# Two attention blocks, forward and backward: K and V loads from SyncE's queue to GpSimd's, dO*O from GpSimd to VectorE

## The chip, the core and the metric

The kernel runs on one core of a Trainium2 chip. The metric is device time in microseconds of one execution. The five engines that matter here are TensorE (PE in the profile; PEld are its weight loads), VectorE (DVE), ScalarE (ACT), GpSimd (POOL) and SyncE (SP, which computes nothing and issues DMAs). Each engine works through its own list of instructions in order. A DMA is issued by SP or by POOL and then carried by the core's DMA engines; a DMA that must wait, for a buffer or for data, holds up what stands behind it on the engine that issues it.

## The reference

Two independent attention blocks, A and B, each with its own x, K cache, V cache, wq and wo. The outputs are the two results side by side and the gradients of all ten inputs.

```python
def block(x, k_cache, v_cache, wq, wo):      # x 8x96x640, caches 8x32x512x128, all bf16
    q = (x @ wq).reshape(B, Sq, H, Dh).transpose(0, 2, 1, 3)
    scores = einsum("bhqd,bhkd->bhqk", q, k_cache) * Dh ** -0.5
    p = softmax(scores)
    o = einsum("bhqk,bhkd->bhqd", p, v_cache)
    return o.transpose(0, 2, 1, 3).reshape(B, Sq, H * Dh) @ wo
out, vjp = jax.vjp(lambda *inputs: concatenate([block(A...), block(B...)]), *inputs)
return out, *vjp(grad_out)
```

There are 8 batch rows (B), 96 queries (Sq), 32 heads (H), 512 keys (Sk) and 128 columns a head (Dh), so a block has 256 pairs of head and batch row, and the kernel 512. For each pair the forward pass needs S = QK^T, P = softmax(S), O = PV; the backward pass needs dV = P^T dO, dP = dO V^T, dS = P * (dP - rowsum(dO * O)), dQ = dS K and dK = dS^T Q. K and V are read once, 64 MB for each block, and dK and dV are written once.

## The kernel before

The kernel is a software pipeline written out by hand. Time is counted in ticks, and each tick starts one pair of head h and batch row b: pair b of head h has the base tick `ct = c0t + b`, with `c0t = tick0 + 8 h`. Block B follows block A without a break in the count. The function `build_block` puts every piece of work into a list with a tick and, inside the tick, a slot; the list is sorted by both and emitted in that order. The table `OFF` (L45) says how many ticks before or after `ct` a piece is due, and `SLOTS` (L51) its place inside the tick. A scheduler may then still move instructions of an engine, except those wrapped in `pinned(...)`, which keep the order of the program on their engine. The softmax pieces have a raised priority.

What one pair goes through:

- `c_ld` (L262) loads K and V. One load brings two batch rows (NB = 2), 256 KB, so K and V have one load each every two ticks. All are issued by SP. K's tile `K_sb` has 7 buffers and is due at tick -5 from its first row's `ct`; V's tile `V_sb` has 5 and is due at tick -3. Both stand in slot 0, the first of the tick. A buffer can be loaded again when its last reader is done: for K the dQ matmuls, 8 ticks after `ct`, for V the O matmuls, 5 ticks after it.
- `c_xt` (L272) transposes a tile on the way, by a DMA that SP issues. V always goes this way (`VT`, 4 buffers, tick 0). K goes this way (`KT`, 2 buffers, tick -3) for half of the pairs; for the others, and for the first heads, `k_on_pe` (L548) leaves it to TensorE: `c_s1` (L280) makes four transposes at tick +2, and VectorE copies the result (`KT_pe`).
- `c_s2a` and `c_s2b` (L291, L304), tick +3: S on TensorE, its row maximum `negm` on VectorE, the exponential `E_sb` on ScalarE.
- `c_s3a` and `c_s3b` (L315, L324), tick +3: `rinv` on VectorE, then `P_sb` on POOL, pinned.
- `c_s4` and the second half of `c_s45` (L382, L352), tick +4: dV, and the four transposes of P, which ScalarE copies to `PT_sb`.
- the first half of `c_s45`, tick +5: O, four matmuls with V; ScalarE copies it into `OD`, together with the dQ of another pair.
- `c_s5b` (L401), tick +5, slot 54: `prod`, the product of O and dO for this pair, 128 x 96, on POOL, pinned.
- `c_s6` (L411), tick +6: dP, with `VT`; `dl_ps`, the sum of `prod` over its 128 rows, by a matmul with ones; then `dS_sb` on VectorE from both and P.
- `c_s7`, tick +7: dK; `c_s8` (L333): four transposes of dS at tick +7 (`dst_ps`, copied to `dST_sb` by VectorE), dQ at tick +8.
- `c_st` (L395): the stores of dV and dK, two batch rows each, issued by POOL, pinned, slot 54.3. One of the two falls on each tick.

Around the pairs there is work per head, spread over the eight ticks of a head: wq and wo tiles loaded by POOL (`pA`, `pA2`, slot 54.6), their transposes, q and dO of the head, dwo and dwq with their stores from POOL, and for every six heads the output projections. At the start of block B, SP also loads x and grad_out once more in row blocks (`ld_tmp`, L118, pinned).

So POOL's list in a plain tick is: P_sb, prod, one store. SP's list is: the loads and the DMA transposes in one order, plus the row blocks.

Of the kernel before, what the change touches and what calls it, by code (L numbers as in the profile page):

```python
# [8 lines left out]
ALU = mybir.AluOpType  # L9
# [32 lines left out]
SL_GRP = 95  # L42
SL_SETUP = 96

OFF = dict(ldk=-5, ldv=-3, kt=-3, vt=0, s2=3, s3=3, s4=4, s5=5, s6=6, s7=7, s8=8)  # L45
HK = dict(pA=-10, pA2=-9, pB=-3, pC0=[-2, 0], pC1=[-1, 0], pD1=1, pD0=2, qA0=18, qA1=17, qB=[19, 20], qD=[(18, 0, 2), (19, 2, 4), (21, 4, 5)])
EV = dict(pB0="act", pB1="dve", pC00="act", pC01="act", pC10="act", pC11="dve", pD0="dve", pD1="dve", qA0="act", qA1="dve", qB0="act", qB1="dve", qD="dve", gU="act")
GSPREAD0 = 9
# [2 lines left out]
SLOTS = dict(LOAD=0, S2A=5, S2B=5.5, S1=6, S8=10, S7=20, S5=30, S4=40, S6=50, S3A=52, S3B=53, S5B=54, HEAD=SL_HEAD, GRP=SL_GRP)  # L51


def build_block(tc, em, tick0, blk, x, kc, vc, wq, wo, g_all, out_all, dx, dk, dv, dwq, dwo, ident, ones, pools, HG=6, first=True, groups=None):
    nc = tc.nc
# [7 lines left out]
    KC = Sk // 128  # L63
    NB = 2
# [46 lines left out]
    def pinned(ins):  # L111
        return tc.keep_in_program_order(ins)
# [149 lines left out]
    def c_ld(h, b, n, bufs):  # L262
        def f():
            src = kc if n == "K" else vc
            X = kvp.tile([128, NB, KC, 128], BF16, name=n + "_sb", bufs=bufs)
            nc.sync.dma_start(X[:], src[b:b + NB, h].rearrange("b (p c) d -> p b c d", c=KC))
            for i in range(NB):
                st = CS.setdefault((blk, h, b + i), {})
                st[n + "_sb"], st[n + "_all"] = X[:, i], X
        return f  # L270
# [130 lines left out]
    def c_s5b(h, b):  # L401
        def f():
            st = CS[(blk, h, b)]
            hs = HS[(blk, h)]
            tok = slice(b * Sq, (b + 1) * Sq)
            prod = wk.tile([128, Sq], BF16, name="prod", bufs=3)
            pinned(nc.gpsimd.tensor_tensor(prod[:], hs["OT_h"][:, tok], hs["dOT_h"][:, tok], op=ALU.mult))  # L407
            st["prod"] = prod
        return f

# [141 lines left out]
    for g in range(NG):  # L552
        h0 = GH0[g]
        for hh in range(groups[g]):
            h = h0 + hh
# [16 lines left out]
            for b in range(B):  # L572
                ct = c0t + b
                if b % NB == 0:
                    em.add(tick0 - 12 if first and h == 0 and b == 0 else ct + OFF["ldk"], SLOTS["LOAD"], c_ld(h, b, "K", 7))
                    em.add(ct + OFF["ldv"], SLOTS["LOAD"], c_ld(h, b, "V", 5))
                    if not k_on_pe(h, b):
                        em.add(ct + OFF["kt"], SLOTS["LOAD"] + 1, c_xt(h, b, "KT", 2))
                    em.add(ct + OFF["vt"], SLOTS["LOAD"] + 1, c_xt(h, b, "VT", 4))
                if k_on_pe(h, b):  # L580
                    em.add(ct + 2, SLOTS["S1"], c_s1(h, b))
                em.add(ct + OFF["s2"], SLOTS["S2A"], c_s2a(h, b))
                em.add(ct + OFF["s2"], SLOTS["S2B"], c_s2b(h, b))
                em.add(ct + OFF["s3"], SLOTS["S3A"], c_s3a(h, b))
                em.add(ct + OFF["s3"], SLOTS["S3B"], c_s3b(h, b))
                em.add(ct + OFF["s5"], SLOTS["S5B"], c_s5b(h, b))
                if b % 2 == 1:
                    em.add(ct + OFF["s4"] + 1, 54.3, c_st(h, b, "v"))
                    em.add(ct + OFF["s7"] + 1, 54.3, c_st(h, b, "k"))
                em.add(ct + OFF["s4"], SLOTS["S4"], c_s4(h, b))  # L590
                for i, o in enumerate(("s8", "s7", "s5", "s4")):
                    SX.setdefault(ct + OFF[o], [None] * 4)[i] = (blk, h, b)
                em.add(ct + OFF["s6"], SLOTS["S6"], c_s6(h, b))
                em.add(ct + OFF["s7"], SLOTS["S7"], c_s7(h, b))
# [147 lines left out]
```

## Time and profile before

| what | value |
|---|---|
| runs | 1696.48, 1707.16, 1713.74 us; median 1707.16 |
| profiled execution, first to last instruction | 1699.8 us |
| mean granted TensorE clock | 0.998 |
| bytes moved by DMA | 423.05 MB, 249 GB/s |
| K and V loads | 512 of 256 KB, median 4.9 to 5.3 us from issue to landing |
| DMA transposes | 256 of V (median 6.1 us to landing), 122 of K (5.2 us) |
| dK and dV stores | 512 of 256 KB |
| prod on POOL | 512 of 360 ns |
| P_sb on POOL | 512 of 689 ns |

The profile is of one execution. "Span" is the time from its first to its last instruction; the runs are whole executions without the profiler. A page gives busy time by engine, the chain of work that ended last, and groups of instructions by source line, with their count, total and mean time and the idle time in front of them. In "L329 POOL P_sb" the number is the line of the kernel. An arrow in "out<-in" names what an instruction writes and reads; an arrow after a waiting instruction names what ended its wait. A DMA issued by POOL is listed as an instruction of POOL, and its time there is the time that POOL needs to issue it, not the time of the transfer; "to landing" runs from the issue to the arrival of the last byte.

### The profile page before, as it was taken

The numbers are of one execution on the slowest core, as the hardware profiler recorded it, in microseconds if no ns is written. First come the engines' busy times: TensorE is split into PE (matmuls) and PEld (weight loads), VectorE is DVE, ScalarE is ACT, GpSimd is POOL, SyncE is SP. The second block draws the span as 40 slices with busy tenths as digits, with TensorE's granted clock in tenths as the row PEclk, the third lists the DMA queues.
The fourth block names the chain that finished last, engine by engine and source line by source line (L and its number), as shares of the span: only waits on it lengthen the run. The fifth ranks groups of instructions, "written<-read, shape, count | busy, mean of one in ns | idle before, by whom it ended". The sixth has DMA issues, their size and how long they took to land.

```text
span 1699.8 us, 56567 instructions
## 1 busy us (share of the span) xinstructions
PE 1675.7 (99%) x22024; PEld 1343.8 (79%) x22024; DVE 1329.8 (78%) x3052; ACT 1405.2 (83%) x3518; POOL 1040.3 (61%) x1747
## 2 busy tenths in 40 slices
PE   8999999999999999999999999999999999999999
PEld 7877778778778778777778877887788778778876
DVE  6887678878788878787778876787788778878877
ACT  6998889869869869878768998897799679878975
POOL 3676567646647647656566764675576557656754
PEclk9999999999999999999999999999999999999999
DMA  9999999999999999999999999999899989999994
GB/s 256 252 259 250 258 225 260 262 242 243 262 221 252 268 238 259 225 251 237 281 256 269 273 270 248 238 289 248 218 261 276 237 221 261 281 217 240 263 247 141
DMA packets 600429, 423.05 MB, mean 249 GB/s; under 512 B 419360, under 2 KB 557984, under 8 KB 600160
## 3 DMA queue, kind: packets, MB, share of 16 engines
q1 hardware_dynamic: 546576, 242.08, 72.2%
q0 software_dynamic: 53584, 177.35, 32.7%
q8 instruction: 173, 2.83, 0.7%
q14 instruction: 96, 0.79, 0.2%
HBM read 161.09 MB, written 159.12 MB: 188 GB/s over the span
## 4 chain that ended last, share of the span: by engine, by line
PE 89%; DMA 4%; ACT 3%; issue 1%; DVE 1%; POOL 0%; SPq 0%; DVEq 0%; ACTq 0%; POOLq 0%
PE q_ps L243 12%; PE o_ps L512 12%; PE dwo_ps L470 6%; PE dV_ps L389 6%; PE dK_ps L432 6%; PE S_ps L298 6%; PE dP_ps L417 6%; PE dwq_ps L490 6%; PE x_ps L340 5%; PE x_ps L365 5%; PE dst_ps L346 5%; PE x_ps L359 5%; PE kT_ps L285 3%; PE n_ps L258 3%; PE nat_ps L455 2%; DMA VT<-V_sb 1%
## 5 line engine op out<-in xcount | busy, mean ns | idle before, releaser
L329 POOL TENSOR_SCALAR P_sb<-E_sb,rinv 96x512 bf16<-96x512 bf16 x512 | 352.6, 689 | 567.8 <-DVE rinv L320 559.2
L310 ACT ACTIVATE E_sb<-S_ps,negm 96x512 bf16<-96x512 f32 x512 | 351.0, 686 | 187.6 <-DVE negm L300 181.9
L421 DVE SCALAR_TENSOR_TENSOR dS_sb<-dP_ps,dl_ps,P_sb 96x512 bf16<-96x512 f32 x512 | 382.1, 746 | 60.9 <-PE dl_ps L419 54.6
L300 DVE TENSOR_REDUCE negm<-S_ps 96x1 f32<-96x512 f32 x512 | 347.6, 679 | 50.9 <-PE S_ps L298 46.6
L435 ACT ACTIVATE dK_sb<-dK_ps 128x512 bf16<-128x512 f32 x512 | 302.1, 590 | 63.4 <-PE dK_ps L432 56.5
L392 ACT ACTIVATE dV_sb<-dV_ps 128x512 bf16<-128x512 f32 x512 | 311.6, 609 | 0.0
L378 ACT ACTIVATE PT_sb<-x_ps 128x384 bf16<-128x384 bf16 x512 | 253.1, 494 | 0.0
L512 PEld LDWEIGHTS <-OD 128*128 128x128 bf16 x1536 | 132.2, 98 | 100.4 <-issue 1.0
L398 POOL DMA_DIRECT2D out_dram<-dV_sb x256 | 194.9, 761 | 11.8 <-issue 8.6
L398 POOL DMA_DIRECT2D out_dram<-dK_sb x256 | 195.0, 762 | 9.1 <-issue 4.4
L389 PE MATMUL dV_ps<-dOnat_h,P_sb 96*128 96x128 bf16 x2048 | 198.2, 219 | 0.8 <-DVE dOnat_h L160 0.6
L417 PE MATMUL dP_ps<-VT,dOT_h 128*96 128x512 bf16 x512 | 195.4, 382 | 3.0 <-DMA VT<-V_sb 3.0
L432 PE MATMUL dK_ps<-Qnat_h,dS_sb 96*128 96x128 bf16 x2048 | 198.1, 219 | 0.1
L407 POOL TENSOR_TENSOR prod<-OD,dOT_h 128x96 bf16<-128x96 bf16 x512 | 184.2, 360 | 13.8 <-ACT OD L375 12.6
L348 DVE COPY dST_sb<-dst_ps 128x384 bf16<-128x384 bf16 x512 | 177.1, 346 | 10.5 <-PE dst_ps L346 10.3
L365 PE MATMUL x_ps<-ident,P_sb 96*128 96x96 bf16 x2048 | 172.0, 205 | 0.8 <-POOL P_sb L329 0.3
L359 PE MATMUL x_ps<-PT_sb,V_sb 128*128 128x96 bf16 x2048 | 172.3, 206 | 0.2 <-ACT PT_sb L378 0.2
L346 PE MATMUL dst_ps<-ident,dS_sb 96*128 96x96 bf16 x2048 | 172.3, 206 | 0.2 <-DVE dS_sb L421 0.2
L340 PE MATMUL x_ps<-dST_sb,K_sb 128*128 128x96 bf16 x2048 | 171.0, 206 | 1.3 <-ACT dK_sb L435 0.8
L375 ACT ACTIVATE OD<-x_ps 128x192 bf16<-128x192 f32 (+1 forms) x515 | 167.9, 326 | 3.9 <-PE x_ps L340 3.9
L320 DVE RECIPROCAL rinv<-rowsum 96x1 f32<-96x1 f32 x512 | 79.9, 156 | 106.0 <-ACT E_sb L310 100.4
L340 PEld LDWEIGHTS <-K_sb 128*128 128x128 bf16 x2048 | 131.1, 98 | 25.1 <-issue 1.6
(84 smaller groups left out, 3744.4 us busy)
## 6 DMA issues: line engine op xcount, KB each, us to landing
out_dram<-dV_sb POOLq DMA_DIRECT2D x256, 256.0 KB, 5.2
out_dram<-dK_sb POOLq DMA_DIRECT2D x256, 256.0 KB, 5.3
K_sb<-in_A_k_cache_dram SPq DMA_DIRECT2D x128, 256.0 KB, 5.3
V_sb<-in_A_v_cache_dram SPq DMA_DIRECT2D x128, 256.0 KB, 5.2
K_sb<-in_B_k_cache_dram SPq DMA_DIRECT2D x128, 256.0 KB, 5.0
V_sb<-in_B_v_cache_dram SPq DMA_DIRECT2D x128, 256.0 KB, 4.9
out_dram<-dwo_sb POOLq DMA_DIRECT2D x63, 160.0 KB, 4.8
out_dram<-dwq_sb POOLq DMA_DIRECT2D x31, 320.0 KB, 6.1
```

The costliest lines, as they stand in the source:

```text
L300: nc.vector.tensor_reduce(negm[:], S_ps[:], axis=AX.X, op=ALU.max, negate=True)
L310: nc.scalar.activation(E_sb[:], st["S_ps"][:], ACT.Exp, bias=st["negm"][:], scale=1.0, accum_out=rowsum[:])
L329: pinned(nc.gpsimd.tensor_scalar(P_sb[:], st["E_sb"][:], st["rinv"][:], 0.0, op0=ALU.mult, op1=ALU.add))
L340: nc.tensor.matmul(dQT_ps, st["K_sb"][:, c, :], st["dST_sb"][:, c * Sq:(c + 1) * Sq], start=(c == 0), stop=(c == KC - 1))
L389: nc.tensor.matmul(dV_ps[:, c * 128:(c + 1) * 128], P_sb[:, c * 128:(c + 1) * 128], hs["dOnat_h"][:, b * 128:(b + 1) * 128], start=True, s ...
L392: nc.scalar.activation(SB[(blk, h, b // 2, "v")][:, b % 2], dV_ps[:], ACT.Identity, scale=1.0)
L398: pinned(nc.gpsimd.dma_start(dst[b - 1:b + 1, h].rearrange("b (p c) d -> p b (c d)", c=KC), SB.pop((blk, h, b // 2, which))[:]))
L417: nc.tensor.matmul(dP_ps[:], hs["dOT_h"][:, tok], st["VT"], start=True, stop=True)
L421: nc.vector.scalar_tensor_tensor(dS_sb[:], dP_ps[:], dl_ps[:, 0:1], st["P_sb"][:], op0=ALU.subtract, op1=ALU.mult)
L432: nc.tensor.matmul(dK_ps[:, c * 128:(c + 1) * 128], dS_sb[:, c * 128:(c + 1) * 128], hs["Qnat_h"][:, b * 128:(b + 1) * 128], start=True, s ...
L435: nc.scalar.activation(SB[(blk, h, b // 2, "k")][:, b % 2], dK_ps[:], ACT.Identity, scale=1.0)
L512: nc.tensor.matmul(o_ps[:], src[:, t * 128:(t + 1) * 128], rhs, start=(hh == 0), stop=(hh == groups[g] - 1))
```

## The change

The K and V loads are issued by POOL, pinned, instead of SP; the loads of head 0 of block A alone stay on SP and in slot 0. The others go from slot 0 to slot 54.4, that is, behind P_sb and the store of their tick and ahead of the wq and wo loads. V's loads are due at tick -4 instead of -3, K's stay at -5. `prod` is computed by VectorE and is not pinned. Which K tiles TensorE transposes does not change, nor do the numbers of buffers.

```diff
-OFF = dict(ldk=-5, ldv=-3, kt=-3, vt=0, s2=3, s3=3, s4=4, s5=5, s6=6, s7=7, s8=8)
+OFF = dict(ldk=-5, ldv=-4, kt=-3, vt=0, s2=3, s3=3, s4=4, s5=5, s6=6, s7=7, s8=8)
...
             X = kvp.tile([128, NB, KC, 128], BF16, name=n + "_sb", bufs=bufs)
-            nc.sync.dma_start(X[:], src[b:b + NB, h].rearrange("b (p c) d -> p b c d", c=KC))
+            v = src[b:b + NB, h].rearrange("b (p c) d -> p b c d", c=KC)
+            if first and h == 0:
+                nc.sync.dma_start(X[:], v)
+            else:
+                pinned(nc.gpsimd.dma_start(X[:], v))
...
             prod = wk.tile([128, Sq], BF16, name="prod", bufs=3)
-            pinned(nc.gpsimd.tensor_tensor(prod[:], hs["OT_h"][:, tok], hs["dOT_h"][:, tok], op=ALU.mult))
+            (nc.vector.tensor_tensor(prod[:], hs["OT_h"][:, tok], hs["dOT_h"][:, tok], op=ALU.mult))
...
                 if b % NB == 0:
-                    em.add(tick0 - 12 if first and h == 0 and b == 0 else ct + OFF["ldk"], SLOTS["LOAD"], c_ld(h, b, "K", 7))
-                    em.add(ct + OFF["ldv"], SLOTS["LOAD"], c_ld(h, b, "V", 5))
+                    sl = SLOTS["LOAD"] if first and h == 0 else 54.4
+                    em.add(tick0 - 12 if first and h == 0 and b == 0 else ct + OFF["ldk"], sl, c_ld(h, b, "K", 7))
+                    em.add(ct + OFF["ldv"], sl, c_ld(h, b, "V", 5))
```

## The prediction

> **What bounds the kernel now.** I read the page first, then the chain of waits stretch by stretch, then the list of who waits for whom, then SyncE's own waits. The page:
>
> ```profile
> span 1699.8 us, 56567 instructions
> ...
> PE 1675.7 (99%) x22024; PEld 1343.8 (79%) x22024; DVE 1329.8 (78%) x3052; ACT 1405.2 (83%) x3518; POOL 1040.3 (61%) x1747
> ...
> DMA  9999999999999999999999999999899989999994
> ...
> PE 89%; DMA 4%; ACT 3%; issue 1%; DVE 1%; POOL 0%; SPq 0%; DVEq 0%; ACTq 0%; POOLq 0%
> ```
>
> TensorE carries 89% of the chain that ended last. Its 99% busy alone would prove little, because a lone matmul's row holds its latency too (219 ns for 128 columns). But in the chain four matmuls of 128 columns take 0.22 us, 0.055 us each, so they run back to back. At that rate (2.4 columns a ns) all 22024 matmuls, each with its columns from the table of groups, take 1574 us. From each matmul's start to the next one's I summed what exceeds this: 121 us in the whole span. Nearly every stretch of 50 us holds 2 to 3.5 us of it, which no queue can give back. Five stretches hold more: 0 to 50 us 12.7 (start), 100 to 150 6.9, 150 to 200 4.5, 750 to 800 6.2, 800 to 850 9.4. Over 2.6 us, the last four together hold 16.6 us, 1.0% of the span: what better transfers could bring at most in this execution. The waits in them:
>
> ```profile
> PE dP_ps L417 <- DMA VT<-V_sb: 3.0, 2, 2.4
> ...
> PE tp_ps L134 <- DMA ld_tmp<-in_grad_out_dram: 2.7, 1, 2.7
> ...
> PE S_ps L298 <- DMA KT<-K_sb: 2.1, 1, 2.1
> ```
>
> Each row: microseconds in total, times, longest. TensorE waited 3.0 us for V's transposes (VT) and 2.1 us for K's, of 378 such transfers, and 2.7 us for a row block of grad_out where block B begins. Two of these stalls have a tail. After the VT wait that ended at 125.3 us the clock falls (stage, then its time, the busy times of PE, PEld, DVE, ACT and POOL, the granted clock, DMA):
>
> ```profile
> 125.00:130.00 5.00, 4.67 (x39) 3.69 (x40) 2.64 (x4) 1.59 (x3) 0.00 (x0) 0.66 1.16 311
> ```
>
> 0.66 over 5 us is 1.7 us lost. The stage 829 to 834 us, after the wait for grad_out, shows 0.66 too: 1.7 us more.
>
> SyncE issues loads and transposes in one order, and stands in it:
>
> ```profile
> SPq L275 <- DMA K_sb<-in_A_k_cache_dram: 169.4, 57, 9.0
> ```
>
> A K transpose waits there for its K tile (152.0 us more for block B's), and the next loads and V transposes wait behind it. VT lands 0.04 to 24.9 us ahead of its matmul, 11.9 in the median: enough nearly always.
>
> **The change part by part.** *Loads leave SyncE.* 504 of 512 loads (all but head 0 of block A) go to POOL. SyncE then holds the transposes and a few row blocks only, with nothing ahead of them but their own tile. On POOL a K load now follows P_sb and the dK store of tick -5, a V load P_sb and the dV store of tick -4: K on odd ticks, V on even ones, one load a tick. The mean tick is 3.24 us (P_sb from 15.3 to 1671.6 us, 511 steps). P_sb ends 3.3 us after its tick's S_ps starts and the store takes 0.76, so a load goes out about 4.1 us into the tick. K then has 8 ticks less that, 22 us, before S_ps (median before 20.6, least 8.7); V 18.6 us before S_ps of its first batch (before 15.7, least 2.9). The loads' own waits should already be over: K's buffer is freed by the dQ matmuls and V's by the O matmuls of the same tick; around 802 us these end at 802.1 and 802.7, and that tick's P_sb only at 804.25. I give back the VT and KT stalls in full, 5.1 us, with the clock's 1.7. The row blocks at B's begin meet fewer loads on SyncE but the same 16 DMA engines; their waits (2.7, and 0.9 for x) and the other 1.7 of clock are 5.3, of which I take half, 2.6 (bounds 0 and 5.3). Gain: 9.4 us.
>
> *POOL.* A load of 256 KB costs POOL what a store of that size does, and the product goes:
>
> ```profile
> L398 POOL DMA_DIRECT2D out_dram<-dV_sb x256 | 194.9, 761 | 11.8 <-issue 8.6
> L407 POOL TENSOR_TENSOR prod<-OD,dOT_h 128x96 bf16<-128x96 bf16 x512 | 184.2, 360 | 13.8 <-ACT OD L375 12.6
> L320 DVE RECIPROCAL rinv<-rowsum 96x1 f32<-96x1 f32 x512 | 79.9, 156 | 106.0 <-ACT E_sb L310 100.4
> ```
>
> 504 x 0.761 = 384 us come, 184 go: 1040 becomes 1240 us, 73%. The plain tick is 0.69 + 0.76 + 0.76 = 2.2 us of 3.24; ticks with a wq, wo, dwo or dwq transfer (0.57 to 0.89, four of the eight ticks of a head) reach 2.8 to 3.1 and still fit. P_sb idled 559 us for rinv, 1.1 a tick, and ends 1.2 us (median; 0.64 at the lowest 5%) before its transposes start. By time alone POOL costs nothing.
>
> But POOL's DMAs also wait for each other. In the trace its 713 DMAs use eight completion semaphores in turn, 89 or 90 on each, and each names its own among its waits: a DMA goes out only when the eighth before it has landed. Now eight span 1699.8 x 8/713 = 19 us. What the two store groups' own view says of landing (least, median, most, in us):
>
> ```profile
> DMA to landing us min/median/max: 2.5/5.2/11.9
> ```
>
> The longest is short of 19, so nothing waits now. With 1217, eight span 11.2 us, and where ticks hold three DMAs 8.6. Behind a waiting load stand wq and wo, the next P_sb, then its transposes and dV on TensorE. Counting, at each moment, the transfers under way that would be POOL's (present issues and landings), 3.9 are out on average and eight or more 0.9% of the time: 15 us. P_sb's idle time and slack take part of it: bounds 0 and 15; I take a third, 5, since both are near a microsecond and a landing that is late by more is rare.
>
> *prod on VectorE.* The trace has no such instruction. It costs more than the reciprocal (156 ns, almost no elements) and less than the sum of 128 columns from PSUM into out_acc (278 ns): 200 ns, nearer the first for its 96 columns of bf16. 512 x 0.2 = 102 us on VectorE, 1330 to 1432, 84%. O's copy ends about as dS starts (median 0.4 us after), so prod lands behind dS, ahead of the next negm, which follows dS at once in 313 ticks; dl_ps needs it 1.5 us (median) after its present end. That is covered by the slack of S_ps to P_sb, except where TensorE already stands on VectorE: dst's transposes start within 0.15 us of dS's end in 45 of 512 ticks. 45 x 0.2 = 9 us if prod always stands ahead there, 0 if never; I take 4.5. It can't gain: dl_ps follows dP in TensorE's order, and prod is ready at least 0.34 us before it today.
>
> One thing no row shows: no VectorE instruction of this kernel reads two SBUF tensors, and P_sb on POOL never varies (685 to 704 ns). The Trainium skill (SBUF — State Buffer, "Who interferes with whom") says that a VectorE instruction with two SBUF inputs and a GpSimd one that reads SBUF hold a shared port in turn, the later blocked for the whole of the other; prod and P_sb are such a pair, and an estimate by it is up to 0.69 us more for a prod that starts just after P_sb.
>
> Sum: -9.4 + 5 + 4.5 = 0.1 us. Against the profiled execution that is 1699.8; the runs' median stands 7.4 above that span, so 1707.
>
> **The rivals.** *Slower: POOL stands on landings.* One mechanism, at the load's wait for the eighth DMA before. Seven of the transfers that would be POOL's are out 4.8% of the time now. If landings grow by a fifth, so that nearly one more is out on average, these moments count too: 5.7%, 97 us, and a third of it, as above, is 32 us: 1739. With two fifths the moments with six (12%) count as well: 17.7%, 300 us, a third 100, 1807. It decides from a median landing of about 6.2 us. For it: loads and stores now share one queue, and the DMA row is at 9 tenths in nearly all slices. Against it: the bytes are the same, and loads issued once a tick are more even than SyncE's bursts.
>
> *Faster by over 1%: the transfers were the whole spread.* All 16.6 us come back and prod and POOL cost nothing: 1690.6. For it: the three runs spread over 17 us though the matmuls are the same in each, and late transfers would do that. Against it: dK's copy waiting for a store (3.1 us) is part of the 16.6, and the change does not help it.
>
> *Hidden anyway.* The stalls are chance and come elsewhere: only the costs are left, 1707 + 9.5 = 1717, still within 1%.
>
> **How the numbers follow.** No change to speak of (my sum, and hidden anyway, ends 1690 to 1724): 0.46. Slower, by the landings or by prod in more ticks than 45: 0.36. Faster by all: 0.18. A measurement of this kernel tells about 1%. The range: 1686 below, where little of the faster case is left out; above, up to 1765, which takes in the fifth and half of the way to two fifths. About 0.1 lies above it and 0.08 below.
>
> **What would show it.** Right: no wait of dP_ps for VT or of S_ps for KT, SyncE's waits now for V and K tiles alone, P_sb still waiting for rinv, POOL near 1240 us, prod near 200 ns behind dS, stores landing near 5.2 us. Wrong: idle time on POOL before DMAs of K_sb and V_sb that a DMA ended, P_sb late and its transposes waiting for it, landings over 6.2 us (the slower rival); VectorE rows with prod well above 278 ns, or E_sb waiting longer for negm than its 181.9 us (prod undercosted).

## The result, and the profile after

| | runs | median us | span of the profiled execution |
|---|---|---|---|
| before | 1696.48 to 1713.74 | 1703.21 | 1699.8 |
| after | 2421.73 to 2514.71 | 2462.38 | 2476.5 |

The change makes the kernel slower by 43%: the ratio is 1.4265, 95% interval [1.4144, 1.4385]. That is far outside the range of the prediction. Every ratio in this text leaves out runs that were disturbed (two of the four after, the profiled one among them), so it need not be the quotient of the medians. The page of the kernel after (its lines stand four higher: S_ps is L302, dP_ps L421, the DMA transposes L279, the loads L270, the stores L402, prod L411):

```profile
span 2476.5 us, 56357 instructions
...
PE 1876.4 (76%) x22024; PEld 1459.8 (59%) x22024; DVE 1423.4 (57%) x3564; ACT 1440.2 (58%) x3518; POOL 1227.5 (50%) x1739
...
DMA  9999999999999999999999999999999999999996
...
DMA packets 503658, 423.02 MB, mean 171 GB/s; under 512 B 419360, under 2 KB 428960, under 8 KB 503392
...
q0 software_dynamic: 93904, 309.51, 58.3%
q1 hardware_dynamic: 409488, 109.92, 53.5%
...
DMA 69%; PE 24%; DVE 2%; ACT 2%; issue 2%; POOL 1%; SPq 0%; DVEq 0%; ACTq 0%; POOLq 0%
DMA KT<-K_sb 36%; DMA VT<-V_sb 25%; DMA out_dram<-dK_sb 6%; PE o_ps L516 4%; PE q_ps L243 3%; PE S_ps L302 2%; PE dwq_ps L494 2%; PE dwo_ps L474 2%; PE dP_ps L421 1%; PE dK_ps L436 1%; PE dV_ps L393 1%; PE dst_ps L350 1%; PE x_ps L344 1%; PE x_ps L369 1%; PE x_ps L363 1%
```

The queues' rows of before:

```profile
q1 hardware_dynamic: 546576, 242.08, 72.2%
q0 software_dynamic: 53584, 177.35, 32.7%
```

The same 423 MB are moved, the DMA engines are as busy as before in every slice, but they move 171 GB/s instead of 249. TensorE's 89% of the chain has become 24%, and DMA's 4% has become 69%. q0 is the queue that POOL issues into, q1 that of SP (each row: packets, MB, share of 16 engines' span). The chain by line names KT<-K_sb with 36% and VT<-V_sb with 25%, both of them DMA transposes. They have stayed on SP, on a queue that the change has emptied of nearly everything else. TensorE's granted clock is lower as well, 0.879 against 0.998, and its matmuls are busy 1876.4 us instead of 1675.7. That is a smaller part: with 24% of the chain on TensorE, an estimate from these shares and clocks gives the clock some 70 us of the loss. The waits, with microseconds in total, times and longest:

```profile
PEld L302 <- DMA KT<-K_sb: 390.8, 77, 12.1
PE S_ps L302 <- DMA KT<-K_sb: 374.7, 77, 11.8
...
PE dP_ps L421 <- DMA VT<-V_sb: 136.1, 62, 5.2
```

Before, S_ps waited 2.1 us for KT in all and dP_ps 3.0 us for VT. V's transposes in their own view (issue time least, median, most in ns; then from issue to landing in us), first before and then after:

```profile
L275 SPq DMA_TRANSPOSE VT<-V_sb x256: 1231/1440/6143, 12.2 to 1656.9; - x128
...
DMA to landing us min/median/max: 3.1/6.1/14.9
```

```profile
L279 SPq DMA_TRANSPOSE VT<-V_sb x256: 1231/5497/14045, 12.0 to 2432.7; - x128
...
DMA to landing us min/median/max: 3.5/18.7/29.6
```

The least values are nearly the same: an undisturbed transpose costs what it did. SP's timeline in a stretch of the middle (start, duration):

```profile
970.85 10.46 SPq L279 DMA_TRANSPOSE VT<-V_sb  x1
981.41 5.16 SPq L279 DMA_TRANSPOSE KT<-K_sb  x1
986.67 18.70 SPq L279 DMA_TRANSPOSE VT<-V_sb  x2
1005.47 3.99 SPq L279 DMA_TRANSPOSE KT<-K_sb  x1
```

SP issues one transpose after another and each takes 4 to 10 us to go out. Over the whole trace, a transpose that is issued with none or one of its kind under way goes out in 1.2 to 1.6 us (median), with two or three under way in 5.9 to 6.1. This reads as if SP's queue took new work only as fast as the engines finish the last; no run tests that reading by itself. Summed over the trace, SP spends 2044 of 2476 us in issuing its 378 transposes (600 us before), and at least one transpose is under way for 2381 us (1533 before). The bulk transfers are slow too: a dV store lands in 13.3 us (median; 5.2 before), a K load in 13.0 to 13.8 (4.9 to 5.3).

The queues' rows put a price on it. The share of q0 times the span, 58.3% of 2476.5 us, is 1444 us of all 16 engines for 309.51 MB, 4.7 us a MB; before it was 32.7% of 1699.8 for 177.35 MB, 3.1 us a MB. The typical packet is not slower (256 B of a transpose: median 18 ns in both kernels; 4096 B of a POOL transfer: 165 ns in both), but the slow ones are: at the 95th percentile 28 ns became 202, and 382 became 1194.

What else the prediction had named, in the kernel after:

```profile
L402 POOL DMA_DIRECT2D out_dram<-dV_sb x256 | 195.3, 763 | 81.9 <-DMA out_dram<-dK_sb 39.7 <-DMA K_sb<-in_A_k_cache_dram 11.6 <-DMA V_sb<-in_A_v_cache_dram 10.4
L411 DVE TENSOR_TENSOR prod<-OD,dOT_h 128x96 bf16<-128x96 bf16 x512 | 119.3, 233 | 70.8 <-ACT OD L379 70.6
L324 DVE RECIPROCAL rinv<-rowsum 96x1 f32<-96x1 f32 x512 | 78.7, 154 | 72.2 <-ACT E_sb L314 66.2
```

POOL does stand on landings now, before its stores and loads. Eight of its DMAs are out 27% of the time. It is the symptom that the prediction had set for its slower rival, and the experiments had to tell whether it is the cause.

### The profile page after: what moved, and what is told of

Same layout as the page of the kernel before. It is cut to its first block, busy times and chain, and to the rows that moved or that the text cites. A ratio compares the mean times of both kernels' runs of the same rounds, so it can differ in the third digit from the quotient of the medians.

```text
span 2476.5 us, 56357 instructions
## 1 busy us (share of the span) xinstructions
PE 1876.4 (76%) x22024; PEld 1459.8 (59%) x22024; DVE 1423.4 (57%) x3564; ACT 1440.2 (58%) x3518; POOL 1227.5 (50%) x1739
## 3 DMA queue, kind: packets, MB, share of 16 engines
q0 software_dynamic: 93904, 309.51, 58.3%
## 4 chain that ended last, share of the span: by engine, by line
DMA 69%; PE 24%; DVE 2%; ACT 2%; issue 2%; POOL 1%; SPq 0%; DVEq 0%; ACTq 0%; POOLq 0%
DMA KT<-K_sb 36%; DMA VT<-V_sb 25%; DMA out_dram<-dK_sb 6%; PE o_ps L516 4%; PE q_ps L243 3%; PE S_ps L302 2%; PE dwq_ps L494 2%; PE dwo_ps L474 2%; PE dP_ps L421 1%; PE dK_ps L436 1%; PE dV_ps L393 1%; PE dst_ps L350 1%; PE x_ps L344 1%; PE x_ps L369 1%; PE x_ps L363 1%
## 5 line engine op out<-in xcount | busy, mean ns | idle before, releaser
L302 PE MATMUL S_ps<-KT,QT_h 128*96 128x512 bf16 x244 | 111.8, 458 | 378.3 <-DMA KT<-K_sb 374.7
L421 PE MATMUL dP_ps<-VT,dOT_h 128*96 128x512 bf16 x512 | 211.4, 413 | 139.5 <-DMA VT<-V_sb 136.1
L302 PEld LDWEIGHTS <-QT_h 128*96 128x96 bf16 x512 | 67.4, 132 | 415.4 <-DMA KT<-K_sb 390.8
L402 POOL DMA_DIRECT2D out_dram<-dV_sb x256 | 195.3, 763 | 81.9 <-DMA out_dram<-dK_sb 39.7
L402 POOL DMA_DIRECT2D out_dram<-dK_sb x256 | 195.5, 764 | 53.8 <-DMA out_dram<-dV_sb 37.3
L436 PE MATMUL dK_ps<-Qnat_h,dS_sb 96*128 96x128 bf16 x2048 | 213.5, 231 | 0.9 <-issue 0.6
L393 PE MATMUL dV_ps<-dOnat_h,P_sb 96*128 96x128 bf16 x2048 | 211.6, 229 | 1.2 <-DVE dOnat_h L160 0.8
L369 PE MATMUL x_ps<-ident,P_sb 96*128 96x96 bf16 x2048 | 183.2, 214 | 20.0 <-POOL P_sb L333 16.0
L363 PE MATMUL x_ps<-PT_sb,V_sb 128*128 128x96 bf16 x2048 | 187.5, 215 | 3.9 <-issue 2.8
L350 PE MATMUL dst_ps<-ident,dS_sb 96*128 96x96 bf16 x2048 | 184.0, 215 | 3.7 <-ACT dK_sb L439 1.5
L344 PE MATMUL x_ps<-dST_sb,K_sb 128*128 128x96 bf16 x2048 | 183.7, 216 | 2.2 <-ACT PT_sb L382 0.9
L344 PEld LDWEIGHTS <-K_sb 128*128 128x128 bf16 x2048 | 142.4, 104 | 32.3 <-issue 6.7
## 6 DMA issues: line engine op xcount, KB each, us to landing
out_dram<-dV_sb POOLq DMA_DIRECT2D x256, 256.0 KB, 13.3
K_sb<-in_A_k_cache_dram POOLq DMA_DIRECT2D x124, 256.0 KB, 13.8
```

Source lines behind the costliest of these rows:

```text
L344: nc.tensor.matmul(dQT_ps, st["K_sb"][:, c, :], st["dST_sb"][:, c * Sq:(c + 1) * Sq], start=(c == 0), stop=(c == KC - 1))
L393: nc.tensor.matmul(dV_ps[:, c * 128:(c + 1) * 128], P_sb[:, c * 128:(c + 1) * 128], hs["dOnat_h"][:, b * 128:(b + 1) * 128], start=True, s ...
L402: pinned(nc.gpsimd.dma_start(dst[b - 1:b + 1, h].rearrange("b (p c) d -> p b (c d)", c=KC), SB.pop((blk, h, b // 2, which))[:]))
L421: nc.tensor.matmul(dP_ps[:], hs["dOT_h"][:, tok], st["VT"], start=True, stop=True)
L436: nc.tensor.matmul(dK_ps[:, c * 128:(c + 1) * 128], dS_sb[:, c * 128:(c + 1) * 128], hs["Qnat_h"][:, b * 128:(b + 1) * 128], start=True, s ...
```

## The experiments

The theory: transposes on one queue and bulk transfers on another get in each other's way inside the 16 DMA engines, and the change put 1.7 times as many bytes on the other queue (309.51 against 177.35 MB). The first rival is that of the prediction, POOL's eight DMAs in turn. A second is the size of the packets: POOL's loads go out in packets of 4096 B, SP's in packets of 1024 B. Beside these, prod on VectorE had to be priced alone. Times without an interval are one execution; beside e4, e5 and e6 the kernel before is one execution too.

| run | what it is | us | before beside it |
|---|---|---|---|
| e1 | the change, prod left on POOL | 2381.81 | 1703.65 |
| e2 | prod on VectorE alone | 1722.37, ratio 1.0102 [1.0054, 1.015] | 1703.65 |
| e3 | the change, copies for transposes | 1713.07 | 1703.65 |
| e4 | the change, loads on ScalarE's queue, prod on POOL | 1803.18 | 1694.79 |
| e5 | the change, all K on TensorE | 1907.31 | 1694.79 |
| e6 | V loads alone on POOL | 1874.1 | 1694.79 |
| e7 | the change, loads in 2-KB rows | 2445.6 | 1701.72 |
| e8 | prod as a one-input reduction on VectorE | 1729.3, ratio 1.0185 [1.0106, 1.0264] | 1701.72 |
| e9 | before, stores on SP's queue | 1688.42, ratio 0.9926 [0.989, 0.9961] | 1701.72 |
| e10 | before, memsets added on VectorE | 1725.64, ratio 1.0039 [0.9992, 1.0086] | 1708.38 |
| e11 | prod on VectorE, a tick later | 1769.09, ratio 1.0383 [1.033, 1.0436] | 1708.38 |
| e12 | loads on POOL, stores on SP | 1876.53 | 1708.38 |
| e15 | before, a reduction added on VectorE | 1726.62, ratio 1.0132 [1.0082, 1.0182] | 1709.18 |
| e16 | prod on VectorE with priority | 1737.31, ratio 1.0184 [1.0142, 1.0226] | 1709.18 |
| e18 | before, V loads at tick -4 | 1705.51, ratio 1.0006 [0.9968, 1.0044] | 1709.18 |

### The parts of the change

**e1, the loads alone.**

```diff
-            (nc.vector.tensor_tensor(prod[:], ...))
+            pinned(nc.gpsimd.tensor_tensor(prod[:], ...))
```

> The change with the product dO*O left on GpSimd. Mixing or lane theory: 2350 to 2550 us, as the change. If the product on VectorE were the cause: about 1710 us.

It measured 2381.81 us. Its chain:

```profile
DMA 65%; PE 27%; POOL 3%; issue 2%; ACT 2%; DVE 1%; SPq 0%; DVEq 0%; POOLq 0%; ACTq 0%
```

The loads carry the loss: 678 us, of the 759 between the medians of after and before (726 by the ratio).

**e2, prod alone,** on the kernel before.

```diff
-            pinned(nc.gpsimd.tensor_tensor(prod[:], ...))
+            (nc.vector.tensor_tensor(prod[:], ...))
```

> The kernel before with only the product moved to VectorE. Mixing or lane theory: 1690 to 1720 us, prod 190 to 200 ns. If the product were the cause: over 2000 us.

The price is 18.7 us between the medians (by the interval 9 to 26), a little above the 1690 to 1720 us that were expected. The chain and prod's own view (least, median, most in ns):

```profile
PE 66%; ACT 13%; DVE 11%; issue 6%; DMA 3%; POOL 0%; ACTq 0%; SPq 0%; DVEq 0%; POOLq 0%
```

```profile
L407 DVE TENSOR_TENSOR prod<-OD,dOT_h x512: 183/198/689, 20.6 to 1699.5; 128x96 bf16<-128x96 bf16 x171
...
  ACT OD L375: 37.9, 97
```

The median is the 200 ns that the prediction took. But 203 of the 512 took over 250 ns, and 202 of these run beside a P_sb on POOL; the longest is as long as a P_sb, 689 ns. The last line is VectorE's idle time before prod, 37.9 us in 97 waits for O's copy. VectorE and ScalarE together now hold 24% of the chain, where they held 4%.

**e18, V loads a tick earlier,** still from SP.

```diff
-OFF = dict(ldk=-5, ldv=-3, kt=-3, vt=0, ...)
+OFF = dict(ldk=-5, ldv=-4, kt=-3, vt=0, ...)
```

> The kernel before with one part of the change alone: V loads at tick -4 in place of -3, still on SyncE's queue (the computation is the reference's). By the forecast's step the 5.1 us of waits for transposes and 1.7 us of clock come back only with the loads off SyncE's queue; the earlier V load alone gives V 3 us more room: 0.996 to 1.002 of the kernel before. Rival: K and V loads and both transposes now come together on one tick of SyncE's queue, and the waits for KT grow by as much as VT's fall, or more: 1.002 to 1.01.

Nothing that can be measured, as the first theory had it.

### Transfers by themselves

Three kernels leave out all of the attention and issue only DMAs, 16 of 256 KB of each kind in a stage (loads in rows of 4 KB: 8 of 512 KB), with a barrier between stages:

```python
def stage(*fs):
    tc.strict_bb_all_engine_barrier()
    for i in range(16):
        for f in fs: f(i)
stage(tran)                                       # SBUF to SBUF transposes, on SP
stage(lambda i: load(nc.gpsimd, i), tran)         # loads on POOL beside them
stage(lambda i: load(nc.sync, i), tran)           # loads on SP in one queue with them
```

> No attention in it: ten stages behind barriers, 16 transfers of 256 KB of each kind a stage; the outputs hold nothing but parts of one cache. Mixing theory (loads on GpSimd's queue and DMA transposes on SyncE's disturb each other on the DMA engines): loads alone some 12 us, transposes alone some 20 to 25 us, both from two queues clearly more than the sum (over 45 us), both from SyncE's one queue about the sum or less, stores on GpSimd's queue beside transposes less than loads there. Lane theory (the transfers go at their usual rate, GpSimd merely waits for its eighth DMA before): two queues take no more than the sum of the two alone, about 35 us, and about the same as one queue.

> No attention in it: stages of 16 transfers of 256 KB of a kind behind barriers, as in the first such kernel (there: loads on GpSimd beside transposes 49.6 us, loads and transposes on SyncE 33.6, loads on ScalarE beside transposes 38.9, loads and stores on GpSimd beside transposes 72.4, loads on SyncE, stores on GpSimd and transposes 48.4). Any second ring hurts: loads on ScalarE with stores on GpSimd beside transposes near 70 us, all three on SyncE well under 48. The size of the other queue's packets hurts (4096 bytes on GpSimd, 1024 before): loads in rows of 4096 bytes from ScalarE beside transposes near 50 us, as from GpSimd, and loads in rows of 1024 bytes on ScalarE with stores on GpSimd under 60. GpSimd's software queue hurts by itself: rows of 4096 bytes from ScalarE stay near 39 us.

> No attention in it: stages of 16 transfers of 256 KB of a kind, as before. If GpSimd's loads hurt the transposes because each packet of 4096 bytes is gathered from four rows of 1024: beside transposes, rows of 1024, 2048 and 4096 bytes take near 50, some 42 and 37 us; with stores beside them near 72, some 64 and 58. If the rows don't matter (the 37 us of rows of 4096 bytes seen before being due to their fewer, larger transfers): 48 to 50 us with rows of 2048. Plain copies in the place of the transposes, with loads and stores on GpSimd: under 45 us, against 72 with transposes.

Measured, from the first issue of a stage to its last landing:

| stage | us |
|---|---|
| 16 transposes alone (SP) | 23.8 |
| 16 loads alone: POOL, SP, ScalarE | 16.0, 14.8, 15.1 |
| loads and transposes, both SP | 33.6 |
| loads ScalarE, transposes SP | 38.9 |
| loads POOL, transposes SP | 49.6 (51.3 again) |
| stores POOL, transposes SP | 43.8 |
| loads POOL, plain copies SP | 26.4 |
| loads POOL in rows of 2 KB, transposes SP | 47.9 |
| loads in rows of 4 KB and transposes SP: from POOL, ScalarE, SP | 37.4 (43.0 again), 38.5, 35.5 |
| 16 plain copies alone (SP) | 12.6 |
| loads and stores POOL, nothing beside them | 28.4 |
| loads and stores POOL, plain copies SP | 37.7 |
| loads and stores POOL, transposes SP, with the loads in rows of 1, 2 and 4 KB | 72.4 (73.2 again), 66.4, 62.3 |

Loads and transposes mixed in one queue take 33.6 us, less than one after the other (14.8 + 23.8 = 38.6). From POOL's queue the same loads beside the same transposes take 49.6, more than one after the other (39.8): running them side by side is worse than not overlapping them at all. With plain copies in place of the transposes the loss is gone: 26.4 us, less than one after the other (16.0 + 12.6). There is no computation here. POOL does wait for its own earlier DMAs in some stages, but it issues the same loads beside the copies, so the loss arises where loads and transposes meet.

The packets' size alone is not the cause: in rows of 4 KB ScalarE's loads go out in packets of 4096 B too, and take 38.5 us beside the transposes where packets of 1024 B take 38.9.

The three kinds together can be held against the kernels. The third column is what the kernel's 423.05 MB would take at the rate of the stage (48 x 262144 B in its time), an estimate that takes a third of the bytes as transposes, where the kernel has 23% (378 of 256 KB):

| loads, stores, transposes | 16 of each, us | 423.05 MB at that rate, us | kernel of that form | its span, us |
|---|---|---|---|---|
| SP, SP, SP | 47.2 | 1587 | e9 | 1686.6, TensorE 91% of the chain |
| SP, POOL, SP | 48.4 (46.1 again) | 1627 | before | 1699.8, TensorE 89% |
| POOL, SP, SP | 56.5 | 1900 | e12 | 1874.8 |
| ScalarE, ScalarE, SP | 46.5 | 1563 | none | |
| ScalarE, POOL, SP | 60.4 | 2031 | e4 | 1801.4 |
| POOL, POOL, SP | 72.4 (73.2 again) | 2434 | e1; after | 2380.0; 2476.5 |

Four of the five kernels fit: where the transfers need less than about 1690 us, TensorE sets the time, and above it the transfers do. How closely they fit is in part luck, since the stages hold more transposes than the kernel. For e4 the stage is too gloomy by 230 us.

One row goes against the theory as it was put: with all loads and stores on ScalarE's queue and the transposes on SP's, a stage takes 46.5 us, no more than with everything on SP's (47.2). So two queues alone are not enough for a loss. The stages that lose much all have POOL's queue among theirs, and the most is lost with loads and stores both on it.

### The transposes in the kernel

**e3, copies for transposes.** The DMA transposes become plain copies of the same size, from SBUF to SBUF, on the same queue; K and V are not transposed there.

```diff
-            nc.sync.dma_start_transpose(XT[:], ...)
+            nc.sync.dma_start(XT[:].rearrange("p a k -> p (a k)"), ...)
```

> The change with each DMA transpose replaced by a plain SBUF to SBUF copy of the same 256 KB from SyncE; S of half the pairs and dP are then computed from tiles that aren't transposed. Mixing theory, the transposes' small packets being what is held up: under 1800 us, GpSimd's transfers landing in 4 to 7 us. Lane theory: GpSimd's list and its waits are the same, so over 2200 us, landings over 10 us.

The chain, and a store's row:

```profile
PE 67%; DVE 11%; ACT 8%; issue 6%; POOL 3%; DMA 3%; ACTq 0%; DVEq 0%; SPq 0%
```

```profile
L402 POOL DMA_DIRECT2D out_dram<-dV_sb x256 | 195.8, 765 | 4.9 <-issue 2.6 <-DVE dS_sb L425 2.3
```

1713.07 us, with every load, store and copy on the queues of the change and POOL at 1227.7 us. The loads of K and V, the stores of dK and dV and the copies land within 4.4 us in the median, eight of POOL's DMAs are out 0.04% of the time, and its stores wait for no landing. This settles the first rival: POOL's work and its eight DMAs in turn cost nothing as long as the transfers are quick. They wait because the transfers are slow. One caution: plain copies are also lighter work for the engines, 12.6 us for 16 of them against 23.8 for 16 transposes, so a part of what e3 gives back is this.

**e5, fewer transposes.** All K tiles go to TensorE, so 256 of 378 DMA transposes remain.

```diff
-        return (b // NB) % 2 == 0 or h == 0 or (first and h == 1)
+        return True
```

> The change with all K transposes on TensorE: 256 DMA transposes instead of 378, 59 us of matmuls more at most. Mixing theory: the time falls with the transposes; from 31.5 us for 16 loads and 16 stores and 72.4 with 16 transposes, a tick costs 1.97 + 0.5 x 2.56 + 0.2 for the rest = 3.45 us, 1770 us, or 2080 scaled as the change's own 2400 stands to its 4.06 a tick. Lane theory: GpSimd's list is the change's own, 2350 us or more.

1907.31 us at 205 GB/s, between the two estimates. A third of the transposes away gives back 555 of the 759 us between the medians, although TensorE has more to do. The transposes of V that are left land in 4.9 us in the median (18.7 after), with every load and store still on POOL.

**e6, fewer loads on POOL.** Only V loads go to POOL; K's stay on SP in slot 0 (prod on POOL).

```diff
-            if first and h == 0:
+            if n == "K" or (first and h == 0):
```

> The change with only V's loads on GpSimd (K's stay on SyncE in slot 0, the product on GpSimd). Mixing theory: half of the loads mix with the transposes, about half of the loss: 1900 to 2200 us. Lane theory: eight DMAs of GpSimd span 8/965 of the time, 14 us and more, over the landings of before: 1700 to 1730 us.

1874.1 us, chain:

```profile
PE 70%; DMA 23%; ACT 2%; DVE 2%; issue 2%; POOL 1%; SPq 0%; DVEq 0%; ACTq 0%; POOLq 0%
```

Just under the 1900 us that were expected at least. 179 us over the kernel before for half of the loads, 678 for all of them (e1): the loss is not in proportion. Even at half, the transposes are 17% of the chain (VT 12, KT 5).

**e7, rows of 2 KB.** The loads keep their bytes but read 2 KB at a stretch, so that the tiles hold other rows.

```diff
-                pinned(nc.gpsimd.dma_start(X[:], v))
+                h2 = h - h % 2
+                w = src[b + h % 2, h2:h2 + 2].rearrange("h (x s) d -> (h x) (s d)", s=8)
+                pinned(nc.gpsimd.dma_start(X[:].rearrange("p b c d -> p (b c d)"), w))
```

> The change with each load fetching 256 KB in rows of 2048 bytes (two heads of one batch row, next to each other in memory) instead of 1024, so that S, dP, O and dQ are computed from other values. If the rows in a packet matter: clearly under the change, 1850 to 2250 us, transposes landing in 8 to 14 us. If the queue alone matters: 2350 to 2500 us.

2445.6 us, no better. In the stages rows of 2 KB gave little (47.9 against 49.6 to 51.3; with stores 66.4 against 72.4 to 73.2). Rows of 4 KB did better there (37.4 and 43.0), in half as many loads of twice the size, but were not tried in the kernel.

### Which queue

**e4, loads on ScalarE's queue,** prod on POOL.

```diff
-                pinned(nc.gpsimd.dma_start(X[:], v))
+                pinned(nc.scalar.dma_start(X[:], v))
```

> The change with its loads issued by ScalarE instead of GpSimd, and the product left on GpSimd. If any second ring beside the transposes hurts as much: over 2200 us. If it is GpSimd's queue with its packets of 4096 bytes: under 1900 us, transposes landing in under 10 us.

1803.18 us, 108 over the kernel before where e1 is 678 over it. The transposes land as in the kernel before (medians 6.0 us for VT and 5.8 for KT; 6.1 and 5.2 there), and no wait of TensorE for one is left. The chain:

```profile
PE 74%; DMA 9%; DVE 8%; ACT 5%; issue 2%; POOL 1%; ACTq 1%; DVEq 0%; POOLq 0%; SPq 0%
```

So 570 us go with POOL's software queue. That the other 108 are lost between two hardware queues is not shown: the loads now stand in ScalarE's list, where ScalarE idles some 45 us until a transpose has landed, and POOL's prod waits 136.9 us for O's copy (12.6 before).

**e9, nearly everything in one queue.** The kernel before with its stores on SP.

```diff
-            pinned(nc.gpsimd.dma_start(dst[b - 1:b + 1, h]..., SB.pop((blk, h, b // 2, which))[:]))
+            pinned(nc.sync.dma_start(dst[b - 1:b + 1, h]..., SB.pop((blk, h, b // 2, which))[:]))
```

> The kernel before with the stores of dK and dV on SyncE's queue, so that nearly all DMAs share one ring. If a second ring beside the transposes costs the kernel before too: transposes landing in under 5 us, no wait of dP_ps for VT, 1680 to 1700 us. If SyncE then stands on the stores' data ahead of its transposes: over 1710 us.

```profile
span 1686.6 us, 57028 instructions
...
q1 hardware_dynamic: 685840, 376.33, 95.9%
...
PE 91%; ACT 4%; issue 2%; DVE 1%; DMA 1%; POOL 0%; SPq 0%; DVEq 0%; ACTq 0%; POOLq 0%
```

Its ratio of 0.9926 [0.989, 0.9961] makes it the fastest kernel here, 13.3 us under the median of the kernel before. Eight of its ten runs lie between 1687.57 and 1688.94 us, where eleven of the thirteen of the kernel before beside them spread from 1694.3 to 1717.57, as if late transfers made much of that spread. VT lands at least 5.1 us ahead of its matmul (0.04 before), and no wait of TensorE for VT or KT is left. SP also holds the stores now, and still V's transposes land in 5.4 us (6.1 before; under 5 was expected).

**e12, loads and stores with their places swapped.** The change with its stores on SP and prod on POOL.

```diff
-            pinned(nc.gpsimd.dma_start(dst[b - 1:b + 1, h]..., SB.pop((blk, h, b // 2, which))[:]))
+            pinned(nc.sync.dma_start(dst[b - 1:b + 1, h]..., SB.pop((blk, h, b // 2, which))[:]))
```

> The change with prod left on GpSimd, K and V loads on the software queue, and the stores moved to SyncE's queue beside the transposes (the computation is the reference's). It swaps the roles of loads and stores in the kernel before. Theory A (what costs is that most of the kernel's transfers run on another queue than the transposes, the stores' 512 or the loads' 512 alike): the times of the loads alone against the transposes and stores on one queue go by the micro-run, 56.5 us against 72.4 and 48.4 us, so the kernel lies between the two kernels, 1800 to 2100 us. Rival B (loads on the software queue are harmful as such): as in the run of the loads alone, 2300 to 2400 us. Rival C (two queues with half the bytes each are harmless, as in the kernel before): 1680 to 1740 us.

```profile
PE 62%; DMA 26%; ACT 7%; issue 3%; DVE 2%; POOL 0%; SPq 0%; ACTq 0%; DVEq 0%; POOLq 0%
```

1876.53 us, inside theory A's bounds. With 175 MB on POOL's queue it has as many bytes there as the kernel before (177 MB), and still takes 168 us more: loads on POOL's queue beside the transposes cost more than stores do, in the kernel as in the stages (56.5 against 48.4). The price shows in another place than after the change. TensorE waits for no transpose; ScalarE waits for the stores, which stand behind the transposes on SP:

```profile
ACT dK_sb L439 <- DMA out_dram<-dK_sb: 113.4, 47, 7.3
...
ACT dV_sb L396 <- DMA out_dram<-dV_sb: 92.6, 38, 7.5
```

### The price of prod

**e8, no second input.** prod becomes a reduction over one tensor on VectorE; dO is left out of it.

```diff
-            pinned(nc.gpsimd.tensor_tensor(prod[:], hs["OT_h"][:, tok], hs["dOT_h"][:, tok], op=ALU.mult))
+            nc.vector.tensor_reduce(prod[:], hs["OT_h"][:, tok].rearrange("p (q o) -> p q o", o=1), axis=AX.X, op=ALU.max)
```

> The kernel before with the product on VectorE replaced by an instruction that reads O alone (a reduction over an axis of one element), so dO is left out of the row sums. If VectorE's instruction is long because its two inputs in SBUF and P_sb's on GpSimd exclude each other: never over 300 ns, and 1700 to 1712 us. If its own time is the cost: 1716 to 1730 us, as with the product.

```profile
L407 DVE TENSOR_REDUCE prod<-OD x512: 227/239/254, 20.8 to 1701.6; 128x96 bf16<-128x96 bf16 x171
...
  ACT OD L375: 37.9, 97
```

The long ones are gone, as an exclusion between the two engines would have it, but the time is not better. VectorE's time for prod falls only from 133.5 to 123.3 us, since the typical one is longer (239 against 198 ns). The long prods by themselves are not what costs.

**e10, an idle memset for each pair,** prod on POOL.

```diff
+            dum = wk.tile([128, 160], BF16, name="dum", bufs=3)
+            nc.vector.memset(dum[:], 0.0)
```

> The kernel before with prod left on GpSimd and one memset of a 128x160 bf16 tile that nobody reads added on VectorE for each pair (512 more VectorE instructions, at the place in the program where prod is issued; the computation is the reference's). Theory A (the 18.7 us that prod on VectorE costs are the price of any 100 to 230 ns instruction that is put into VectorE's order ahead of dS): about 1.0 to 1.02 of the kernel before, 10 to 30 us more. Rival B (they are the price of its wait for O's copy, 37.9 us by the waits, behind which dS stands; the memset waits for nothing): within 0.3% of the kernel before.

The scheduler drew all 512 memsets into the first 381 us, 54.2 us of VectorE's time. They are not spread over the pairs, so the run answers less than it was meant to. The interval of its ratio, 0.9992 to 1.0086, takes in no change.

**e11, prod a tick later.**

```diff
-                em.add(ct + OFF["s5"], SLOTS["S5B"], c_s5b(h, b))
+                em.add(ct + OFF["s5"] + 1, 11, c_s5b(h, b))
```

> The kernel before with prod on VectorE, as in the run of prod alone, but issued one tick later, behind the place of dS's copies, so that O has been copied out long before (the computation is the reference's). Theory A (any added VectorE instruction costs as much, wherever it stands): again about 1.01 of the kernel before, 1720 us. Rival B (the wait for O's copy and the place ahead of dS make the price): the row of waits prod for OD falls from 37.9 us to under 5 us, and the time is within 0.4% of the kernel before.

Both theories missed. In prod's view, what VectorE waited for before it, and who waited for it:

```profile
  ACT OD L375: 51.5, 138
who waited for it (us, times):
...
  PEld L419: 89.6, 114
  PE dl_ps L419: 53.0, 69
```

The edit did not do what it was for. prod now waited for a later copy into OD, and stood right before dS 213 times of 512 (101 in e2). TensorE waited for it, and the price grew to 3.8%.

**e15, a reduction that nobody needs,** prod on POOL.

```diff
+            dum = wk.tile([128, 1], F32, name="dum", bufs=3)
+            nc.vector.tensor_reduce(dum[0:Sq], st["P_sb"][:, 0:128], axis=AX.X, op=ALU.add)
```

> The kernel before, prod on GpSimd as it was, and one VectorE reduction over 96x128 bf16 of P_sb added for each pair, whose result nobody reads (some 240 ns; it waits for P_sb of its own pair, two ticks old, and never for O; the computation is the reference's). Theory A (prod's price on VectorE is that of any instruction of this length added to VectorE's order, among negm, rinv, dST and dS): 1.008 to 1.02 of the kernel before, 14 to 34 us. Rival B (the price is the wait for O's copy, 37.9 us of VectorE's idle time with prod there): within 0.4% of the kernel before.

```profile
L409 DVE TENSOR_REDUCE dum<-P_sb x512: 261/273/285, 15.1 to 1697.5; 96x1 f32<-96x128 bf16 x171
...
  POOL P_sb L329: 56.7, 149
```

Its time is theory A's. It never waits for O, but the scheduler moved it up to its P_sb, so that VectorE stood 56.7 us for that instead.

**e16, prod with the scheduler's priority.**

```diff
-            pinned(nc.gpsimd.tensor_tensor(prod[:], ...))
+            with tc.high_priority(PRIO_OFF):
+                nc.vector.tensor_tensor(prod[:], ...)
...
-                em.add(ct + OFF["s5"], SLOTS["S5B"], c_s5b(h, b))
+                em.add(ct + OFF["s5"] + 1, 0.5, c_s5b(h, b))
```

> The kernel before with prod on VectorE, issued at tick +6 ahead of that tick's O copy and with the planner's high priority, so that it stands behind dS 305 of 512 times (179 with prod at its place in the change) and needs only the copy of the tick before (the computation is the reference's). Theory A (any instruction of this length costs as much, wherever it stands): 1.008 to 1.02 of the kernel before. Rival B (the wait for O's copy makes the price): the row of waits prod for OD falls from 37.9 us to under 10 us and the time is within 0.5% of the kernel before.

prod still waited 34.3 us for O's copy (37.9 in e2), so the run could not take that wait away. Its time is theory A's.

Together: an instruction of 0.24 to 0.32 us (mean) added for each pair to VectorE costs 1.0 to 1.9%, whatever it computes (e2, e8, e15, e16). Neither the long prods nor the wait for O in particular make the price. Open is how it divides between VectorE's added time and its standing for an input in mid-order, because every one of these instructions brought some such wait (34 to 57 us).

## Why the prediction was wrong

**What bounds the kernel** was read rightly. The stalls on VT and KT were there to be had: e9 has none and gains 13.3 us, between the 9.4 of the sum and the 16.6 of the cap. How much of the 13.3 these stalls make, the run does not tell. The rate of 2.4 columns a ns is a little above what the row in the chain gives (128 columns in 0.055 us are 2.3); the 16.6, a difference between stretches, hardly depends on it.

**Loads leave SyncE: the step that failed.** The working counted when a load is issued and what stands before it on which engine, and took the transfers as given: it kept "the same 16 DMA engines", and against the slower rival it said "the bytes are the same". Both are true, and neither fixes how long the transfers take. The same bytes on the same engines moved at 171 instead of 249 GB/s, because the loads, 132 MB, went to POOL's queue, away from that of the transposes (m1, e1, e3, e4). The sum gave back 5.1 us of waits for VT and KT; after the change TensorE's matmuls wait 511 us for them. The Trainium skill (DMA: Bandwidth & Descriptors, "Issuing engines are not separate DMA queues") says that transfers run on the same 16 engines whoever starts them, and that issuing from several engines saves only issue time. The runs agree for plain transfers (loads and stores on POOL beside copies on SP take 37.7 us, and 28.4 and 12.6 alone) and for loads and stores on ScalarE beside transposes on SP (46.5 us against 47.2 on one queue). They differ where POOL's loads meet transposes: 72.4 us.

The page of before had the warning, in its DMA row: 9 tenths in nearly every slice. The sum used it in the slower rival alone, as a reason for longer landings. It should have been a bound: 423.05 MB in 1699.8 us is 249 GB/s, and the engines were busy throughout to give it. A kernel in that state has little room for a loss of rate: by the estimate from the stages its transfers need 1627 of its 1700 us. It did not follow from the trace how much the rate would lose; the three kinds of transfer were never seen on other queues than their own.

**POOL** was right in size (1240 us forecast, 1227.5 measured) and right in effect: with quick transfers it costs nothing (e3). The term for the eight DMAs in turn had counted 0.9% of the time with eight out, from the landings of before; it is 27% with the landings of after, and 0.04% in e3.

**The slower rival** had the sign and the symptom (landings over 6.2 us, POOL idle before DMAs) but not the mechanism. It put the price on POOL's waits, and the chain has POOL at 1% and the transposes KT and VT at 61%. Its cases of a fifth and two fifths also stop far short of landings that are 2.6 times as long.

**prod on VectorE** has the duration that was forecast (200 ns; 198 in e2, 195 after). The term of 4.5 us with its bounds of 0 and 9 was mis-sized: it measured 18.7. It counted only the 45 ticks in which dst's transposes start right behind dS, and nothing for VectorE's standing in order for O's copy, nor for the next negm and E_sb in all ticks. VectorE's and ScalarE's share of the chain, from 4 to 24% in e2, shows that the cover was thinner than the slack of one wait told. The named sign (E_sb waiting longer for negm than 181.9 us) is there in e2, but small: 193.6.

The port rule was met in its effect: the Trainium skill (SBUF — State Buffer, "Who interferes with whom") has a two-input VectorE instruction and a reading GpSimd instruction exclude each other, and 202 of the 203 long prods lie beside a P_sb, up to its 689 ns, while the one-input form stays at 227 to 254 ns. But the time does not follow from it (e8).

**The parts do not quite add up.** Loads 678 and prod 18.7 are 697 of 759 us between the medians (726 by the ratio). The runs of after spread over 93 us and e1 is one execution, so the rest is not told apart from this spread.

## What to carry to other kernels

Before a transfer changes its queue, look at what runs in the engines beside it. If DMA transposes do, one queue for them and the bulk of the other transfers was the fastest kernel here, ScalarE's queue beside them did as well in a stage, and POOL's queue cost most; the mix can be timed in a few stages of bare DMAs before the kernel is touched. Where the DMA row is at 9 tenths throughout, the kernel may need most of the rate that it has, and what is lost of it shows in the time once the transfers are the longer side. An instruction added to an engine at 78% is not free, though the engine idles a fifth of its time: price it by the path that runs through that engine's order.

## What the runs showed of the hardware

- Loads on POOL's queue beside transposes on SP's lose the engines' time itself. In that stage, in the 30 us that begin 1.5 us after its start, the packets handled (for one of the 16 engines on average 52 of 4096 B and 290 of 256 B), at their undisturbed 165 and 18 ns, account for 14 us. With both on SP's queue it is some 20 of 21 us (packets of 1024 B at 46 ns), and with loads and stores on POOL beside plain copies some 29 of 30 (2048 B at 84 ns).
- How much is lost depends on the queue: loads beside transposes take 33.6 us on the same queue, 38.9 from ScalarE's and 49.6 from POOL's; with stores as well 47.2, 46.5 and 72.4. POOL's loads go out in packets of 4096 B where SP's and ScalarE's are of 1024. The size alone does not make the difference (38.5 us with 4096 B from ScalarE). Whether it is the queue's kind or how a packet is put together from rows is open: from POOL, rows of 2 KB gain little in the stages and nothing in the kernel (e7), and rows of 4 KB (37.4 and 43.0) also came in fewer, larger loads.
- A transpose's issue on SP takes 1.2 us when nothing holds it up, and 5.9 to 6.1 in the median with two or three others under way (after).
- Why the engines lose the time was not settled. The slow packets are a tail and not a shift (median 18 ns in both kernels, mean 31 before and 53 after for the transposes' 256 B), as if an engine stopped now and then between two queues. That is a reading, not a result.
